# Attention and MLP in one kernel: an earlier score round, and the last stores cut into parts

## The chip, the cores and the metric

The kernel runs on one core of one Trainium2 chip, in one launch. The metric is the device time of an execution in microseconds (us). An execution has a span, from the first to the last instruction that the profiler records, and about two microseconds around it.

## The reference

Eight batches, eight heads of 64 channels, 512 local and 32 global tokens a batch. Local queries see the 32 global keys and the local keys within a window of 32 positions; global queries see everything. The heads' outputs are put side by side (544 rows of 512 channels a batch, 4352 in all), and two matrices with a gated activation between them follow.

```python
s_g  = scale * q_g @ concat(k_g, k_l).T ;  out_g = sm(s_g) @ concat(v_g, v_l)
s_ll = where(|i - j| <= 32, scale * q_l @ k_l.T, -1e9)
s_lg = scale * q_l @ k_g.T
out_l = sm(concat(s_lg, s_ll)) @ concat(v_g, v_l)
x = concat(out_g, out_l) as [4352, 512]
h = x @ w_in                      # 512 -> 2048
out = (h * sigmoid(1.702 * h)) @ w_out    # 2048 -> 512, float32
```

## The kernel before

Operands are bf16, sums float32. The order in which each engine works is the order in which the program names the steps; there is no scheduler behind it. Each engine runs its own list, and waits are put in from the tiles that are written and read.

**Attention** of a batch is done in two *quads* of four heads, `a` and `c` in the code (class `Wide` from batch 1 on). A quad has these steps:
- `S(0)`, `S(1)`: the scores in two rounds, 24 matmuls each with 32 rows in use at a time (32*128 in the profile, L558), into four PSUM banks of their own (`psS`). Both rounds and all quads share these four banks, so a round waits for the exponentials of the round before it.
- `X(0)`, `X(1)`: exponentials on ScalarE (L569), two instructions a round, into `e`. `M(0)`, `M(1)`: the window's mask is multiplied in on VectorE, or on GpSimd where the code says so (L574).
- `U(0)`, `U(1)`, `U(2)`: 24 matmuls each, tile shape 128*32 (L584). `U(0)` sums the exponentials, `U(1)` and `U(2)` give the products with the values. Each takes one bank `ov`. `Gm` (20 matmuls, L595) gives the global queries' output into a bank `og`. `UG` is these four in a row.
- `R`: VectorE transposes the sums (`sT`, L460), takes reciprocals (L462) and transposes back (`rs`, L464). `XL(0)`, `XL(1)` multiply the `ov` banks by them into the MLP's input `xL` (L469). `G` does the same for the global rows.

**MLP.** For each batch `h_step` runs 16 times (four matmuls into a bank `hp`, L613, then the activation on ScalarE, L618). The second product is done for batches 2 and up in `Pair`s of two tiles of 128 rows, with seven products of eight matmuls (128*128, L724, `mm(k)`) instead of eight; VectorE and ScalarE put them together (`m3`, `z`, `zm`, `sub`, `evict`, `add`), and `store` writes the rows in eight DMAs from SP's queue (L762). A pair uses two banks, `px` and `py`.

The banks `hp`, `ov`, `og`, `px`, `py` and `op` come in turn from one pool of four (`psP`): each takes the bank that the fourth before it used, once that has been read. In `phase_o` the two pairs and the two quads' steps take them in this order: a's three `ov` and `og`, then `px` and `py` of the first pair, c's three `ov` and `og`, then `px` and `py` of the second pair. So c's third `ov` and its `og` go where the first pair's `px` and `py` were, and the second pair's `px` and `py` go where c's first two `ov` were.

`phase_o(i)` runs for batches 2 to 6 between the `h_step` loops of batch i and i+1. It puts the pairs of batch i between the attention steps of batch i+1, and, for i = 2 to 5, starts the first quad `a2` of batch i+2. This last form (`if a2`) is the one that the change touches, and it runs four times. `loads_after` issues the DMAs of the values and keys of later batches on GpSimd's queue, behind its mask multiply.

**The end.** The rows of the 32 global tokens of all batches (256 rows) go through the MLP last (`h_step(B, ...)`, then the code from L1138). Its seven products go into four banks `x0`, `x1`, `y0`, `y1`; the last product, `mm(7)`, adds into `y0`, which VectorE has read before (L1157). The four results, each 128 partitions by 256 channels, are stored as quarters, one DMA of 128 KB each: the first and the last from ScalarE's queue, the second and third from SP's (L757).

Every store adds to one of eight semaphores, which are given out in turn, and waits first for the store before it on the same semaphore.

Of the kernel before, what the change touches and what calls it, by code (L numbers as in the profile page):

```python
# [20 lines left out]
def kernel(  # L21
# [12 lines left out]
    nc = tc.nc  # L34

    B, H, Sl, D = q_l.shape
    Sg = q_g.shape[2]
# [128 lines left out]
    for i in range(2):  # L166
# [3 lines left out]
        out=step, in_=step, pattern=[[1, 289]], compare_op=ALU.is_ge,  # L170
# [105 lines left out]
    out_by_row = out.rearrange("(b s) m -> s b m", b=B)  # L276
# [6 lines left out]
    def spair():  # L283
        return [psS.tile([128, 2, 512], F32, name="s4", tag="s%d" % i) for i in range(2)]

    def bank(pair, j):
        return pair[j // 2][:, j % 2, :]
# [340 lines left out]
    def gelu_table():  # L628
        gelu(spot[:, 0:1], spot[:, 1:2])

    def exp_table():
        nc.scalar.activation(spot[:, 0:1], spot[:, 1:2], AF.Exp)
# [26 lines left out]
    HM = d_model // 2  # L659
# [18 lines left out]
    def g_sums(i, lo, hi, which=(0, 1, 2, 3)):  # L678
        n = width(i)
        if i not in sums:  # L680
            if i < B:
                sums[i] = [moe.tile([128, FC // 2, w * HT], BF16, name="gs%d" % k)
                           for k, w in enumerate((1, 1, 2, 1))]
            else:
                room = [ld.tile([128, 2, 16 * D], BF16, name=x).rearrange("p a b -> p (a b)")
                        for x in ("rk", "rq", "rk")]
                sums[i] = [x.rearrange("p (g t) -> p g t", g=FC // 2)
                           for x in (room[0][:, :1024], room[0][:, 1024:], room[1], room[2][:, :1024])]
        a11, a12, a21, a22 = parts_of(i)
        t = gTs[i].rearrange("p (g e) t -> p g e t", e=2)  # L690
        g = slice(lo, hi)
        for k in which:
            if k == 2:
                nc.vector.tensor_tensor(sums[i][2][:, g, :n], t[:, g, 0, :n], t[:, g, 1, :n], ALU.add)  # L694
            else:
                x, y, op = {0: (a11, a22, ALU.add), 1: (a21, a11, ALU.subtract), 3: (a12, a22, ALU.subtract)}[k]
                nc.vector.tensor_tensor(sums[i][k][:, g, : n // 2], x[:, g], y[:, g], op)  # L697

    class Pair:
# [53 lines left out]
                tile_out(self.i, self.tt + h * (width(self.i) // 256),  # L753
                         self.ob[:, 2 * h : 2 * h + 2].rearrange("p h m -> p (h m)"))

        def quarter(self, h, m, eng):
            eng.dma_start(out=out_by_row[:Sg, 4 * h : 4 * h + 4, m * HM : m * HM + HM], in_=self.ob[:, 2 * h + m])  # L757

    def tile_out(i, tci, ob):
        rows = out[i * S + Sg : (i + 1) * S].rearrange("(r t) m -> t r m", t=16)  # L760
# [12 lines left out]
    a, c = Quad(0), Quad(1)  # L773
# [86 lines left out]
    a, c = nq[1]  # L860
# [63 lines left out]
    a, c = nq[2]  # L924
# [26 lines left out]
    def loads_after(i):  # L951
        if i + 2 < B:
            load_v(i + 2)
        if i == 1:
            load_g(8, NQ)
        if i + 3 < B:
            load(i + 3)

    def quads_of(n):
        if n < B and n not in nq:  # L960
            nq[n] = (Wide(2 * n), Wide(2 * n + 1))
        return nq.get(n, (None, None))
# [44 lines left out]
    def phase_o(i):  # L1007
        b = i + 1
        a, c = nq[b]
        a2, c2 = quads_of(b + 1)  # L1010
        p0, p1 = Pair(i, 0), Pair(i, 1)
        exp_table()
        a.UG()
        c.S(0)
        a.R()
        g_sums(i, 7, 8, (0,))
        a.XL(0)
        g_sums(i, 7, 8, (1, 2))
        a.XL(1)
        g_sums(i, 7, 8, (3,))  # L1020
        p0.mm(3, 4, 1)
        c.X(0)
        p0.m3()
        p0.z()
        a.G()
        c.M(0)
        c.S(1)
        c.X(1)
        p0.mm(6)
        p0.zm()  # L1030
        c.M(1)
        p0.mm(5, 2)
        p0.sub()
        p0.evict()
        p0.mm(7)
        p0.add()
        p0.store()
        if a2:
            c.U(0)
            a2.S(0)  # L1040
            a2.X(0)
            a2.M(0, nc.gpsimd)
            c.U(1)
            c.U(2)
            c.Gm()
            loads_after(i + 1)
        else:
            pt = spair()
            c.U(0, bank(pt, 0))
            c.U(1, bank(pt, 2))  # L1050
            c.U(2, bank(pt, 3))
            c.Gm(bank(pt, 1))
        c.R()
        c.XL(0)
        if a2:
            c.XL(1)
            c.G()
        p1.mm(3, 4)
        p1.m3()
        p1.z()  # L1060
        if not a2:
            c.XL(1)
            c.G()
        p1.mm(1, 6)
        p1.zm()
        if a2:
            a2.S(1)
            a2.X(1)
        p1.mm(5, 2)
        p1.sub()  # L1070
        p1.evict()
        gelu_table()
        p1.mm(7)
        p1.add()
        if a2:
            a2.M(1)
        p1.store()

    for i in range(1, B):
        if i > 1:  # L1080
            for fc in range(FC):
                h_step(i, fc)
                if i == 2 and fc == 0:
                    weight_sums(1, 2)
                if i + 1 < B:
                    c = nq[i + 1][1]
                    if fc == 1:
                        c.Tk()
                        c.Tq()
                        c.ext((3,))  # L1090
                    if fc in (3, 5, 7):
                        c.ext(((3, 5, 7).index(fc),), on_act)
                    if fc == 9 and i + 2 < B:
                        a2 = quads_of(i + 2)[0]
                        a2.T()
                        transpose_g(2 * i + 4, 2 * i + 6)
                        a2.ext()
                if fc in (4, 8, 12):
                    g_sums(i, fc // 2 - 2, fc // 2)
                if fc == 13:  # L1100
                    g_sums(i, 6, 7)
        if i == 1:
            phase_o1()
        elif i + 1 < B:
            phase_o(i)
# [4 lines left out]
    def pair_banks(k):  # L1110
        return [psX.tile([128, 512], F32, name="x", tag="x%d" % (2 * (k % 2) + j)) for j in range(2)]
# [3 lines left out]
    for st in range(FC):  # L1115
        h_step(B, st)
        if st < len(todo):
            tt, k = todo[st]
            if k == 3:
                p = Pair(B - 1, tt, pair_banks(tt))  # L1120
# [19 lines left out]
    p = Pair(B, 0, (x0, x1, y0, y1))  # L1140
# [7 lines left out]
    p.mm(5)  # L1148
    on_act(p.ob[:, 1], x0[:, :HM])
    nc.vector.tensor_sub(zb, za, x0[:, :HM])  # L1150
    p.quarter(0, 1, nc.scalar)
    p.mm(2)
    on_act(p.ob[:, 2], x1[:, :HM])
    nc.vector.tensor_sub(zc, za, x1[:, :HM])
    p.quarter(1, 0, nc.sync)
    p.mm(1)
    nc.vector.tensor_add(zc, zc, y0[:, :HM])  # L1157
    p.mm(6)
    nc.vector.tensor_add(p.ob[:, 3], zc, y1[:, :HM])
    p.quarter(1, 1, nc.sync)  # L1160
    p.mm(7)
    nc.vector.tensor_add(p.ob[:, 0], zb, y0[:, :HM])
    p.quarter(0, 0, nc.scalar)


# [28 lines left out]
```

## Time and profile before

| | |
|---|---|
| median of 3 runs | 288.9 us (288.88 to 288.94) |
| profiled execution | 288.66 us |
| its span | 286.6 us, 2.06 less than its time |
| granted TensorE clock | 1.0 |
| TensorE busy | 277.6 us, 97% of the span |
| VectorE, ScalarE, GpSimd busy | 204.6, 184.4, 94.1 us |
| one `phase_o` with `a2` (the second) | from 132.33 to about 150.1 us |
| first product of the last rows' end (L724) | from 276.34 us |

In the profile's rows PE is TensorE's matmuls, PEld its weight loads, DVE is VectorE, ACT ScalarE, POOL GpSimd, SP the engine whose queue issues most stores (SPq, and ACTq for ScalarE's queue). A row gives start and length in microseconds, then engine, line, operation, the tile written and the tiles read; in brackets how long the engine had been idle and what ended it. The chain of waits follows the work back from the last instruction; "x24" counts the instructions that were recorded, of which a few can be missing.

### The profile page before, as it was taken

What the parts mean: (1) busy time and instruction counts of PE and PEld (TensorE: products, weight loads), DVE (VectorE), ACT (ScalarE), POOL (GpSimd) and SP (SyncE); (2) the same over time, 40 slices, a digit from 0 to 9 for tenths busy, and PEclk for the clock granted to TensorE, in tenths of its full rate; (3) what the DMA queues carried; (4) which work ended last, traced back from release to release, by engine and by line L of the source; (5) the groups of instructions that cost most, each with busy time, mean ns of one, the idle gap of its engine ahead of it and who ended that gap; (6) DMA issues with size and microseconds to landing.
All of it is one profiled execution on the core that took longest, in us unless ns stands there. A gap on an engine that the chain in (4) does not pass through costs nothing.

```text
span 286.6 us, 8822 instructions
## 1 busy us (share of the span) xinstructions
PE 277.6 (97%) x3704; PEld 178.6 (62%) x3727; DVE 204.6 (71%) x494; ACT 184.4 (64%) x296; POOL 94.1 (33%) x140
## 2 busy tenths in 40 slices
PE   7899999999999999999999999999999999999994
PEld 6544445544554488646884588647874588458883
DVE  7671457788689898679957997779957697363452
ACT  4847657388778784778559774877658761873440
POOL 8974550766936002920086004800040000000000
PEclk9999999999999999999999999999999999999999
DMA  7999994999999802993059703940122003200213
GB/s 204 167 200 211 202 143 66 153 224 144 161 170 174 150 3 57 91 185 59 12 84 160 139 2 78 107 58 5 29 54 70 2 3 76 73 0 2 73 44 106
DMA packets 59543, 28.23 MB, mean 98 GB/s; under 512 B 47472, under 2 KB 50032, under 8 KB 59504
## 3 DMA queue, kind: packets, MB, share of 16 engines
q0 software_dynamic: 51664, 17.57, 55.1%
q1 hardware_dynamic: 7264, 9.31, 11.8%
q10 hardware_dynamic: 576, 0.79, 0.8%
q8 instruction: 29, 0.48, 0.7%
q14 instruction: 10, 0.08, 0.1%
HBM read 36.31 MB, written 8.91 MB: 158 GB/s over the span
## 4 chain that ended last, share of the span: by engine, by line
PE 91%; DVE 2%; DMA 2%; POOL 1%; issue 1%; ACT 1%; DVEq 0%; POOLq 0%
PE hp L613 38%; PE px L724 13%; PE py L724 9%; PE op L653 9%; PE x L724 6%; PE s L558 6%; PE ov L584 5%; PE s L613 2%; DMA rk<-in_k_l_dram 2%; DVE xL L469 1%; ACT e L382 1%; PE og L595 1%; DVE rs L464 1%; DVE sT L460 0%; PE s L354 0%
## 5 line engine op out<-in xcount | busy, mean ns | idle before, releaser
L613 PE MATMUL hp<-xL,w_in_sb 128*128 128x512 bf16 x465 | 104.6, 379 | 1.2 <-DVE xL L469 0.4
L613 PEld LDWEIGHTS <-w_in_sb 128*128 128x128 bf16 x576 | 56.1, 98 | 60.3 <-issue 0.7
L618 ACT ACTIVATE gT<-hp 128x512 bf16<-128x512 f32 x120 | 69.9, 598 | 20.8 <-PE hp L613 19.3
L569 ACT ACTIVATE e<-s 128x1016 bf16<-128x1016 f32 (+1 forms) x56 | 53.3, 1003 | 22.1 <-PE s L558 22.0
L724 PEld LDWEIGHTS <-gs 128*128 128x128 bf16 x480 | 46.2, 98 | 6.4
L697 DVE TENSOR_TENSOR gs<-gT 128x512 bf16<-128x512 bf16 (+1 forms) x90 | 30.4, 365 | 17.6 <-ACT gT L618 17.3
L574 POOL TENSOR_TENSOR e<-e,mask 128x1760 bf16<-128x1760 bf16 x4 | 13.3, 3320 | 82.6 <-ACT e L569 82.6
L98 POOL DMA_DIRECT2D v<-in_v_l_dram x40 | 31.2, 781 | 15.4 <-PE og L595 4.3
L724 PE MATMUL py<-wsum,gs 128*128 128x256 bf16 x240 | 30.3, 273 | 0.0
L574 DVE TENSOR_TENSOR e<-e,mask 128x1712 bf16<-128x1712 bf16 (+1 forms) x24 | 25.2, 1049 | 6.0 <-ACT e L569 5.9
L653 PE MATMUL op<-w_out_sb,gT 128*128 128x512 bf16 x122 | 28.8, 380 | 0.5 <-issue 0.3
L510 DVE STREAM_TRANSPOSE kT<-rk 128x512 f32<-128x512 f32 x14 | 14.6, 1044 | 15.3 <-DMA rk<-in_k_l_dram 15.3
L653 PEld LDWEIGHTS <-gT 128*128 128x128 bf16 x128 | 11.8, 98 | 13.9
L724 PEld LDWEIGHTS <-gT 128*128 128x128 bf16 x192 | 18.0, 98 | 2.7
L724 PE MATMUL px<-w_out_sb,gT 128*128 128x256 bf16 x160 | 19.2, 273 | 0.0
L724 PE MATMUL px<-w_out_sb,gs 128*128 128x256 bf16 x160 | 19.1, 273 | 0.0
L469 DVE TENSOR_TENSOR xL<-ov,rs 128x512 bf16<-128x512 f32 x27 | 17.9, 687 | 0.8 <-PE ov L436 0.4
L694 DVE TENSOR_TENSOR gs<-gT 128x1024 bf16<-128x1024 bf16 (+1 forms) x30 | 17.4, 580 | 0.0
L558 PEld LDWEIGHTS <-kT 32*128 32x128 bf16 x672 | 12.6, 93 | 7.3 <-issue 5.9
L113 ACT ACTIVATE ob<-px 128x512 f32<-128x512 f32 x10 | 6.0, 599 | 15.2 <-DVE zz L746 15.2
L558 PE MATMUL s<-q,kT 32*128 32x160 bf16 (+1 forms) x448 | 14.9, 246 | 0.0
L100 POOL DMA_DIRECT2D v<-in_v_g_dram x24 | 13.9, 580 | 1.8 <-DMA rq<-in_q_l_dram 1.7
(149 smaller groups left out, 343.4 us busy)
## 6 DMA issues: line engine op xcount, KB each, us to landing
out_dram<-ob SPq DMA_DIRECT2D x128, 64.0 KB, 2.3
rq<-in_q_l_dram POOLq DMA_DIRECT2D x5, 512.0 KB, 8.4
rk<-in_k_l_dram POOLq DMA_DIRECT2D x5, 512.0 KB, 10.6
v<-in_v_l_dram POOLq DMA_DIRECT2D x24, 96.0 KB, 4.7
w_in_sb<-in_moe_w_in_dram POOLq DMA_DIRECT2D x8, 256.0 KB, 8.2
w_out_sb<-in_moe_w_out_dram POOLq DMA_DIRECT2D x4, 512.0 KB, 10.4
rq<-in_q_l_dram POOLq DMA_DIRECT2D x5, 256.0 KB, 7.9
rk<-in_k_l_dram POOLq DMA_DIRECT2D x5, 256.0 KB, 7.9
```

What stands on the lines that cost most here:

```text
L98: nc.gpsimd.dma_start(out=vt[0:n, hs, c, :D], in_=vs[FIRST[c] : FIRST[c] + n, hs])
L469: nc.vector.tensor_mul(self.x[:, 2 * self.u + h, :], self.st[1 + h], self.st["rs"])
L510: nc.vector.transpose(flat[:, 0:Sl].rearrange("p (r t) -> p t r", t=16), loaded[self.b][0][:, self.u].bitcast(F32))
L558: nc.tensor.matmul(bank(self.ps, j)[:, at : at + n], lhsT=self.k[p, KEYS[c] : KEYS[c] + 128, e], rhs=qs[p, :, :, e], start=(e == 0), stop= ...
L569: nc.scalar.activation(self.E[rnd][:, 2 * i : 2 * i + 2, :n], self.ps[i][:, :, :n], AF.Exp, scale=scale)
L574: eng.tensor_mul(e, e, mask[:, rnd : rnd + 1, :n].to_broadcast([128, 4, n]))
L613: nc.tensor.matmul(hp[:, : width(i)], lhsT=w_in_c[:, fc // 4, kc, fc % 4 // 2, :, fc % 2], rhs=(xL[i] if i < B else xG)[:, kc, :], start=( ...
L618: nc.scalar.activation(out_, in_, AF.Gelu_apprx_sigmoid)
L653: nc.tensor.matmul(op, lhsT=gTs[i][:, fc, tci * 128 : tci * 128 + 128], rhs=w_out_sb[:, fc, :], start=(first and fc == 4 * f4), stop=(fc = ...
L694: nc.vector.tensor_tensor(sums[i][2][:, g, :n], t[:, g, 0, :n], t[:, g, 1, :n], ALU.add)
L697: nc.vector.tensor_tensor(sums[i][k][:, g, : n // 2], x[:, g], y[:, g], op)
L724: nc.tensor.matmul(out_, lhsT=lv[:, g, tt * 128 : tt * 128 + 128], rhs=rv[:, g, :], start=(g == 0 and k in ((1, 3, 4, 6) if self.apart els ...
```

## The change

`quarter` takes a list of queues and cuts its DMA into as many parts, by rows of each batch's 32 (8 rows in a quarter's part, 16 in a half). The first quarter becomes four parts, all on SP's queue; the second two, both on ScalarE's; the third two, the first on SP's, the second on ScalarE's; the last two, the first on ScalarE's and the second on SP's. In all ten DMAs instead of four.

In `phase_o` with `a2`, `a2.S(0)` and what follows it (`X`, and `M` on GpSimd) stand ahead of all of c's `UG`, instead of between its `U(0)` and `U(1)`. On TensorE the 24 matmuls of `S(0)` come before the 24 of `U(0)`; the order on the other engines stays.

```diff
-        def quarter(self, h, m, eng):
-            eng.dma_start(out=out_by_row[:Sg, 4 * h : 4 * h + 4, m * HM : m * HM + HM], in_=self.ob[:, 2 * h + m])
+        def quarter(self, h, m, *engs):
+            n = Sg // len(engs)
+            for j, eng in enumerate(engs):
+                eng.dma_start(out=out_by_row[n * j : n * j + n, 4 * h : 4 * h + 4, m * HM : m * HM + HM],
+                              in_=self.ob[4 * n * j : 4 * n * j + 4 * n, 2 * h + m])
...
         if a2:
-            c.U(0)
             a2.S(0)
             a2.X(0)
             a2.M(0, nc.gpsimd)
-            c.U(1)
-            c.U(2)
-            c.Gm()
+            c.UG()
             loads_after(i + 1)
...
-    p.quarter(0, 1, nc.scalar)
+    p.quarter(0, 1, *4 * [nc.sync])
...
-    p.quarter(1, 0, nc.sync)
+    p.quarter(1, 0, nc.scalar, nc.scalar)
...
-    p.quarter(1, 1, nc.sync)
+    p.quarter(1, 1, nc.sync, nc.scalar)
...
-    p.quarter(0, 0, nc.scalar)
+    p.quarter(0, 0, nc.scalar, nc.sync)
```

## The prediction

> **What bounds the kernel now.** I read the page first, then the chain of waits in order of time, then the timeline around the two edited places, then the DMA issues.
>
> ```profile
> span 286.6 us, 8822 instructions
> PE 277.6 (97%) x3704; PEld 178.6 (62%) x3727; DVE 204.6 (71%) x494; ACT 184.4 (64%) x296; POOL 94.1 (33%) x140
> PE 91%; DVE 2%; DMA 2%; POOL 1%; issue 1%; ACT 1%; DVEq 0%; POOLq 0%
> ```
>
> TensorE is the bound from end to end; an edit counts only if it shortens TensorE's own row of work, makes it wait, or moves what follows its last matmul. First edit, first of its four places, in the chain (start, length, what):
>
> ```profile
> 108.70 0.87 PE py L724 x8
> 109.57 0.48 PE ov L584 x24
> 110.05 0.58 PE s L558 x22
> 110.63 0.84 PE ov L584 x40
> 111.47 0.16 PE og L595 x20
> 111.63 1.85 PE px L724 x16
> ```
>
> From the end of py to the start of px, TensorE alone takes 2.06 us: U(0), S(0), U(1) and U(2), Gm. The same gap is 2.05 to 2.06 at 141.16, 172.74 and 204.31. The batch-1 phase already has the new order, S then the whole UG:
>
> ```profile
> 74.59 0.57 PE s L558 x24
> 75.17 1.22 PE ov L584 x66
> 76.38 0.16 PE og L595 x17
> 76.54 0.32 PE op L653
> ```
>
> That is 76.54 - 74.59 = 1.95 us. What VectorE does behind these, from the timeline (start, length, engine, line, what):
>
> ```profile
> 110.28 0.71 DVE L460 STREAM_TRANSPOSE sT<-ov 128x512 f32<-128x512 f32 x1
> 111.56 1.92 PE L724 MATMUL px<-w_out_sb,gT 128*128 128x256 bf16 x16
> 112.13 1.29 DVE L469 TENSOR_TENSOR xL<-ov,rs 128x512 bf16<-128x512 f32 x2
> ```
>
> And the end of the kernel:
>
> ```profile
> 280.33 0.39 ACT L113 ACTIVATE ob<-x 128x256 f32<-128x256 f32 x1 [0.74 <-PE x L724]
> 281.27 0.42 DVE L1157 TENSOR_TENSOR ob<-ob,x 128x256 f32<-128x256 f32 x1
> 281.75 0.75 PEld L724 LDWEIGHTS <-rk 128*128 128x128 bf16 x7 [0.18 <-issue]
> 282.82 0.42 DVE L1162 TENSOR_TENSOR ob<-ob,x 128x256 f32<-128x256 f32 x1 [0.60 <-PE x L724]
> 283.27 0.55 ACTq L757 DMA_DIRECT2D out_dram<-ob  x1
> ```
>
> ```profile
> out_dram<-ob SPq DMA_DIRECT2D x8, 64.0 KB, 1.7
> out_dram<-ob ACTq DMA_DIRECT2D x2, 128.0 KB, 2.2
> out_dram<-ob SPq DMA_DIRECT2D x2, 128.0 KB, 2.1
> ```
>
> The last store is issued at 283.27, lands about 2.1 later (285.37), and 1.2 us of closing follow.
>
> **Edit 1, S(0) ahead of all of UG, four phases.** Nothing is added; 24 matmuls move past the 24 of U(0). TensorE changes between its tile shapes (128*128, 128*32, 32*128) four times in this stretch now, three times afterwards. Gain by the rows: 2.06 - 1.95 = 0.11 us a phase, if nothing makes TensorE wait. What could:
>
> S(0) needs the score banks that the exponentials of c's second round leave at 106.01 + 1.89 = 107.90; it starts at 109.50. U(0) needs the mask multiply that ends at 107.93 + 1.05 = 108.98. U(2) and Gm reuse the banks of the first px and py, free at 110.21 (ScalarE's eviction) and 110.36 (VectorE's add); U(2) comes at about 110.86. All covered, by 0.5 us or more. ScalarE's exponentials start at 110.24 instead of 110.66, still behind that eviction, so GpSimd's mask multiply and the v loads queued behind it go 0.4 us earlier; nobody waits for them.
>
> R is the thin place. Its transpose waits for U(0), which now comes one S(0) later. At 81.28 and 75.10, with S in front, the transpose starts 0.60 after U(0)'s first matmul; S to U(0) is 0.57. So it starts at 109.50 + 0.57 + 0.60 = 110.67, not 110.28 (where VectorE itself was busy until then): R and both XL go 0.39 later. The second px goes into U(0)'s bank and waits for that transpose: 110.67 + 0.71 + 0.06 of handover (VectorE ends at 281.69, TensorE goes on at 281.75) = 111.44, against a natural start of 109.50 + 1.95 = 111.45. No wait. The second py goes into U(1)'s bank and waits for XL(0): its start follows the transpose's by 1.85 (112.13 - 110.28), its length is 0.69 where L469 stands alone, so 110.67 + 1.85 + 0.69 + 0.06 = 113.27, against a natural start of 113.32 - 0.11 = 113.21. A wait of 0.06 takes half of the gain. Left: 0.05 to 0.06 a phase, 0.24 us in four. Bounds: 0.11 x 4 = 0.44 gained (no wait); and, if the handover costs 0.16 as the bubble at 48.53 between U and op does, about 0.05 lost per phase, 0.2 in all. VectorE's later z is covered: it idles 0.85 us before zm at 115.27.
>
> **Edit 2, the four quarters.** (a) The first quarter's issue leaves ScalarE, where it takes 0.66 us (279.62 to 280.28) in front of the next eviction. That eviction can follow its matmul by 0.09, as the one at 279.21 does: 280.08 instead of 280.33. VectorE's chain behind it moves by 0.25, L1157 ends at 281.44 instead of 281.69, and the 0.18 us that TensorE stands before its last eight matmuls goes. L1162 ends at 283.07, not 283.24: 0.17 gained at this point.
>
> (b) The stores. In the program as built each store adds to one of eight semaphores, and first waits for the former store on its semaphore. The eight were given out in an order in which ScalarE's two parts of the second quarter stand before the third and fourth part of the first quarter on SP:
>
> ```
> SP   8x4x256   [waits DMAHW1, Activation]   part 1 of first quarter
> SP   8x4x256   [waits DMAHW2]               part 2
> SP   8x4x256   [waits DMAHW4]               part 3
> SP   8x4x256   [waits DMAHW5]               part 4
> SP   16x4x256  [waits DMAHW6, DVE]          half of third quarter
> SP   16x4x256  [waits DMAHW7, DVE]          half of fourth quarter
> ACT  16x4x256  [waits DMAHW4, Activation]   half of second quarter
> ACT  16x4x256  [waits DMAHW5]               other half
> ```
>
> The wait values say that parts 3 and 4 wait until ScalarE's two halves have landed. Queued on SP behind them: half of the third and half of the last quarter, whose landing ends the kernel. The trace of before has such a wait once (SP on an earlier store, 0.9 us). Step by step: ScalarE issues its halves after its eviction, at 280.08 + 0.39 + 0.02 = 280.50. A store of 128 rows took 0.65 to 0.66 to issue as the first of its shape on a queue and 0.54 to 0.55 as the second; one of 32 rows about 0.43; I take 0.58 and 0.47 for 64 rows. Second half issued at 281.08. Landing: 64 KB takes 1.6 to 1.8, 128 KB 2.1 to 2.4; I take 1.80, nearer the first, since the bytes are the same: 282.88. Part 4 then starts at about 282.92, is issued by 283.35, the third quarter's half by 283.95, and the last half is issued at 283.97 although its data is there at 283.07. It lands 1.75 later: 285.72 against 285.37, so **0.35 us later**, with (a) already in it. ScalarE's last half goes at 283.10 and lands before that. SP's first two parts find their semaphores free.
>
> On these halves the Trainium skill speaks against the change (DMA: Bandwidth & Descriptors, section "Rules for kernel authors": two transfers to disjoint partition halves serialize, so use one). By the fit on the same page (about 2.0 us and bytes / 436 GB/s, made on GpSimd's queue) an estimate for 64 KB is 2.15 us; with both landings at that the end would come 1.10 later instead of 0.35, which is the slower rival's side below. The trace's own 64 KB stores, at 1.7, do not agree.
>
> **Sum.** -0.24 + 0.35 = +0.11 us on the profiled execution: 288.66 becomes 288.77. The median of the runs is 0.24 higher (288.9), so 289.0. What a measurement of this kernel can tell from no change is about 0.2%, 0.58 us; this lies inside.
>
> **Rivals.**
> *Slower: halves cost what wholes cost.* One mechanism, SP's wait for ScalarE's landings, at whole-store prices: halves issued from 280.50, 0.66 each step, landing 2.2: 281.16 + 2.2 = 283.36; part 4 0.43; half of the third 0.65; last half issued at 284.50, landing 2.1 later: 286.60, 1.23 late; less 0.24: +1.0, 289.9 us. For it: the fixed part of a store is most of its time (1.7 against 2.2 for half the bytes). Against: the 64 KB rows. It decides the verdict once the two landings together exceed my 3.55 by some 0.5. Chance 0.25.
> *Faster: SP's wait is short and the phases keep their whole gain.* Halves at 32-row prices: second issued at 280.93, landed (1.6) at 282.53; part 4 by 282.98, half of the third by 283.42, last half lands at 285.04: 0.33 early; with 0.44 from the phases -0.77, 288.1 us. Chance 0.13.
> *Phases give nothing:* the dearer handover (0.16) makes the second py late, +0.2 with +0.35: 289.5 us, mostly inside 0.2%. Chance 0.12.
> *It does not do what it says:* the score round does move in the built program; "by both queues" holds only in name, since SP waits for ScalarE's stores. That is in my sum.
>
> **How the numbers follow.** My forecast has 0.5. Of it and the third rival some 0.06 lies above +0.58. Faster: 0.13; slower: 0.25 + 0.06 = 0.31; same: 0.56. The likeliest is 289.0; the range of 288.3 to 289.9 takes in the bounds of the phases and the slow rival's price, and leaves out what lies beyond it and most of the fast rival.
>
> **What the profile after would show.** Right: gaps of 1.95 to 2.01 from py's end to the second px, with a bubble of some 0.05 before the second py; sT about 0.4 later in each phase; ScalarE's last-but-one eviction 0.25 earlier and no 0.18 before the last matmuls; SP's store parts 3 and 4 at about 282.5 and 282.9 (less 0.24 for what came before), SP's last issue later than ScalarE's by 0.9. Wrong: SP's parts follow each other without a break and the last store is issued right behind L1162 (then faster), or the gap is 2.06 or more (then edit 1 gave nothing), or landings above 2.1 us (then slower).

## The result, and the profile after

| | before | after |
|---|---|---|
| median | 288.95 us (14 runs) | 289.76 us (14 runs) |
| ratio after to before | | 1.003, 95% interval 1.002 to 1.004 |
| profiled execution, its span | 288.66, 286.6 us | 291.09, 289.0 us |

The change makes the kernel 0.8 us slower, just beyond what can be told from no change. The profiled execution of after is one of its longest: its batch-2 phase begins 1.53 us later than before (102.28 against 100.75) and its chain at the start runs through loads that the change does not touch. So the two traces are compared piece by piece, each from its own start.

The chain of waits in order of time, first of the four phases (start, length, what):

```profile
110.24 0.87 PE py L724 x8
111.11 0.57 PE s L558 x24
111.69 1.20 PE ov L584 x63
112.89 0.16 PE og L595 x18
113.05 1.85 PE px L724 x16
114.90 1.82 PE py L724 x16
```

From py's end to px's start: 113.05 - 111.11 = 1.94 us instead of 2.06. The 0.12 lies in UG: its `ov` matmuls take 1.20 in one row, and 0.48 and 0.84 where S(0) stands between them. That a change of tile shape less is what saves it fits these rows; no run tests it by itself. The 16 matmuls of py that follow take 1.82 instead of 1.75. The same two figures stand in the other three phases (1.94 and 1.82 in each). Net 0.05 a phase. Counted from the start of the first of the four to the start of the phase behind them, this trace gives less: 228.54 - 102.28 = 126.26 against 227.07 - 100.75 = 126.32, 0.06 in all, partly because the second phase's first `ov` matmuls, which the change does not touch, take 1.29 instead of 1.20. The timeline shows where the 0.07 comes from:

```profile
112.21 0.72 DVE L460 STREAM_TRANSPOSE sT<-ov 128x512 f32<-128x512 f32 x1 [0.32 <-PE ov L584]
...
112.98 1.92 PE L724 MATMUL px<-w_out_sb,gT 128*128 128x256 bf16 x16
...
114.07 1.29 DVE L469 TENSOR_TENSOR xL<-ov,rs 128x512 bf16<-128x512 f32 x2
114.63 1.81 PEld L724 LDWEIGHTS <-gs 128*128 128x128 bf16 x16
114.81 1.91 PE L724 MATMUL py<-wsum,gs 128*128 128x256 bf16 x16
```

R's transpose now waits for U(0) (0.32 us of idling). It starts 1.17 after S(0)'s first matmul (111.04); px is not held up, since the transpose ends at 112.93 and px starts at 112.98. py stands still until XL(0), 0.69 long, is done: 114.07 + 0.69 = 114.76, start 114.81.

The end, first the engines, then the issues of SP one by one, the last of the eight stores ahead (L765) and the six of the quarters (L759):

```profile
280.67 0.38 ACT L113 ACTIVATE ob<-x 128x256 f32<-128x256 f32 x1 [1.41 <-DMA out_dram<-ob]
...
281.50 0.38 ACT L113 ACTIVATE ob<-x 128x256 f32<-128x256 f32 x1 [0.44 <-PE x L724]
281.82 4.90 SPq L759 DMA_DIRECT2D out_dram<-ob  x6
281.91 3.21 ACTq L759 DMA_DIRECT2D out_dram<-ob  x4
...
282.44 0.42 DVE L1157 TENSOR_TENSOR ob<-ob,x 128x256 f32<-128x256 f32 x1
...
284.12 0.42 DVE L1162 TENSOR_TENSOR ob<-ob,x 128x256 f32<-128x256 f32 x1 [0.45 <-PE x L724]
```

```profile
281.29 0.44 SPq L765 DMA_DIRECT2D out_dram<-ob  x1
...
281.82 0.84 SPq L759 DMA_DIRECT2D out_dram<-ob  x1
...
282.71 0.69 SPq L759 DMA_DIRECT2D out_dram<-ob  x1
...
283.95 0.65 SPq L759 DMA_DIRECT2D out_dram<-ob  x1
...
284.65 0.66 SPq L759 DMA_DIRECT2D out_dram<-ob  x1
...
285.42 0.62 SPq L759 DMA_DIRECT2D out_dram<-ob  x1
...
286.14 0.58 SPq L759 DMA_DIRECT2D out_dram<-ob  x1
```

The last data are ready at 284.12 + 0.42 = 284.54. ScalarE issues its half of the last quarter at 284.57. SP issues the other half at 286.14, **1.60 us after the data**; before it was 0.03. The hole between 283.40 and 283.95 is the wait for ScalarE's first half (issued at 281.91), which the view of SP's waits lists:

```profile
SPq L759 <- DMA out_dram<-ob: 0.5, 1, 0.5
```

Part four, which by the program waits for ScalarE's second half, follows part three at once (283.95 + 0.65 = 284.60, start 284.65). The first part does not start when its data are ready, at 280.67 + 0.38 = 281.05, but 0.77 later, right behind the eight stores of the last pair that SP had still to issue (281.29 + 0.44 = 281.73). The prediction does not have this; by these rows it costs nothing here, since part three waits for ScalarE's landing either way.

From the last vector instruction's end to the end of the span: 289.0 - 284.54 = 4.46 us, before 286.6 - 283.24 = 3.36. That is 1.10 more. Ahead of it the pause of 0.18 before the last eight matmuls is gone (the last 24 matmuls take 2.78 instead of 2.95). Sum by the pieces: -0.05 x 4 - 0.17 + 1.10 = +0.73, or +0.87 with the 0.06 that the four phases gave in this trace; measured +0.81.

### The profile page after: what moved, and what is told of

It is laid out like the page before. It is cut to its first block, busy times and chain, and to the rows that moved or that the text cites. A ratio compares the mean times of both kernels' runs of the same rounds, so it can differ in the third digit from the quotient of the medians.

```text
span 289.0 us, 8853 instructions
## 1 busy us (share of the span) xinstructions
PE 280.4 (97%) x3727; PEld 179.8 (62%) x3727; DVE 205.0 (71%) x494; ACT 184.2 (64%) x296; POOL 94.0 (33%) x140
## 4 chain that ended last, share of the span: by engine, by line
PE 89%; DMA 4%; ACT 2%; DVE 2%; SPq 0%; issue 0%; POOL 0%
PE hp L613 36%; PE px L724 13%; PE py L724 9%; PE op L653 9%; PE x L724 6%; PE s L558 6%; PE ov L584 5%; DMA rk<-in_k_l_dram 3%; DMA early<-in_q_l_dram 2%; PE s L613 1%; ACT e L382 1%; PE og L595 1%; PE s L354 1%; ACT e L385 1%; PE s L337 1%; ACT gT L618 0%
## 5 line engine op out<-in xcount | busy, mean ns | idle before, releaser
L653 PE MATMUL op<-w_out_sb,gT 128*128 128x512 bf16 x128 | 29.5, 380 | 0.0
```

The costliest lines, as they stand in the source:

```text
L653: nc.tensor.matmul(op, lhsT=gTs[i][:, fc, tci * 128 : tci * 128 + 128], rhs=w_out_sb[:, fc, :], start=(first and fc == 4 * f4), stop=(fc = ...
```

## The experiments

All times are medians, with the ratio to the kernel before on the same chip and its 95% interval. "End" is the time from the end of the last vector instruction to the end of the span, and "last issue" the time from there to the start of the last store's issue, both from each run's trace.

### Each edit alone

The score round moved, the four stores as before:

```diff
-    p.quarter(0, 1, *4 * [nc.sync])
+    p.quarter(0, 1, nc.scalar)
-    p.quarter(1, 0, nc.scalar, nc.scalar)
+    p.quarter(1, 0, nc.sync)
-    p.quarter(1, 1, nc.sync, nc.scalar)
+    p.quarter(1, 1, nc.sync)
-    p.quarter(0, 0, nc.scalar, nc.sync)
+    p.quarter(0, 0, nc.scalar)
```

> Only the score round is moved; the four stores are as before. Theory (one change of tile shape less on TensorE, half of it given back by py's wait for XL(0)): each of the four phases 0.04 to 0.05 us shorter, the gap from py's end to px's start 1.94, py 0.07 late; 0.2 us less in all, 288.75 against 288.95, which is at the edge of what can be told. Rival (the earlier round costs elsewhere, in the loads or the loops): 289.2 or more.

288.83 us, 0.9994 (0.9984 to 1.0003). The trace has the expected pieces (1.93 to 1.94 from py to px, py 1.82), and the four phases from start to start take 126.17 us, 0.15 less than before. The time agrees with -0.2 but can't be told from nothing, and the rival's 289.2 is out.

The stores alone, the phases as before:

```diff
-            a2.S(0)
...
-            c.UG()
+            c.U(0)
+            a2.S(0)
...
+            c.U(1)
+            c.U(2)
+            c.Gm()
```

> Only the stores are changed; the phases are as before. Theory (the end alone makes the change slower): from the last vector instruction to the end of the span 4.4 to 4.5 us instead of 3.36, the last product 0.17 earlier; 0.9 us more, 289.85. Rival (the moved round is to blame): 289.0.

289.96 us, 1.0036 (1.0023 to 1.005). End 4.45, last issue 1.58 after the data. The stores alone make the kernel as slow as the whole change does, within the intervals.

### What holds SP's last issue back

Whole quarters on swapped queues, both edits otherwise as in the change:

```diff
-    p.quarter(0, 1, *4 * [nc.sync])
-    p.quarter(1, 0, nc.scalar, nc.scalar)
-    p.quarter(1, 1, nc.sync, nc.scalar)
-    p.quarter(0, 0, nc.scalar, nc.sync)
+    p.quarter(0, 1, nc.sync)
+    p.quarter(1, 0, nc.scalar)
+    p.quarter(1, 1, nc.sync)
+    p.quarter(0, 0, nc.scalar)
```

> Both edits, but each quarter stored whole: first on SP, second on ScalarE, third on SP, fourth on ScalarE, four DMAs as before. Theory (the number of issues on SP is what costs, and taking the first issue off ScalarE is worth 0.17): the last store issued right behind the last vector instruction, 3.36 us to the end as before; 0.2 from the phases and 0.17 less, 288.6. Rival (SP's backlog of eight stores holds the first and third quarter up): third quarter issued late, 288.95 or more.

288.73 us, 0.9988 (0.9977 to 0.9999). End 3.40, last issue 0.04 after the data, although SP's first store again starts behind its earlier ones (280.39, its data ready at 279.62). The last 56 matmuls take 6.13 us, and 6.28 in the run with the order alone: moving the first issue off ScalarE takes the pause away in the trace, but the time can't be told from 288.83. So it is not the other queue that made the end late; it is the cut.

The second quarter issued from GpSimd, so that SP waits for no store of ScalarE's:

```diff
-    p.quarter(1, 0, nc.scalar, nc.scalar)
+    p.quarter(1, 0, nc.gpsimd, nc.gpsimd)
```

> As the changed kernel, but the second quarter's two halves are issued from GpSimd, so that no store of SP's waits for a store of ScalarE's; SP still issues its six. Theory of the prediction (SP's wait for ScalarE's landings is most of the delay): the last store issued within 0.2 us of the last vector instruction, some 1.4 us earlier than in the changed kernel, 288.5. Rival (six issues of 0.6 to 0.8 us one after another are most of it, whatever they wait for): SP's six follow each other from 281.8 without a break, the last at about 285.6 instead of 286.14; 0.5 us less than the changed kernel, 289.3.

289.14 us, 1.0004 (0.9996 to 1.0013). The timeline's last vector instruction and SP's six issues:

```profile
281.15 4.38 SPq L759 DMA_DIRECT2D out_dram<-ob  x6
...
283.45 0.42 DVE L1162 TENSOR_TENSOR ob<-ob,x 128x256 f32<-128x256 f32 x1 [0.45 <-PE x L724]
```

Without the wait the six still fill 4.38 us, 0.58 to 0.84 each, and the last starts at 284.96, 1.09 after the data instead of 1.60. The rival was right: the wait is 0.5 of the delay, and the row of six issues, which begins 0.76 after the first quarter's data (280.39), is enough for the rest.

The first quarter's parts cut by batch, everything else as in the change:

```diff
+            if len(engs) == 4:
+                for j, eng in enumerate(engs):
+                    eng.dma_start(out=out_by_row[:Sg, 4 * h + j, m * HM : m * HM + HM],
+                                  in_=self.ob[j : 128 : 4, 2 * h + m])
+                return
```

> As the changed kernel, but the first quarter's four parts are cut by batch (32 rows of one batch each) instead of by rows (8 rows of four batches each); same bytes, queues, number and waits. Theory (an issue's price goes with the pattern, three dimensions against two, and not with the bytes): the first two parts take 0.43 us each to issue instead of 0.84 and 0.69, the last store is issued 0.3 to 0.4 earlier, 289.4. Rival (the price goes with SP and ScalarE issuing at the same time): 0.6 to 0.8 as before, 289.76.

289.87 us, 1.0025 (1.0016 to 1.0035). The same 32 KB now take 0.58, 0.58, 0.47 and 0.47 us to issue instead of 0.84, 0.69, 0.65 and 0.66, so the price goes with the pattern, if less than expected. The time did not move:

```profile
280.60 3.38 SPq L760 DMA_DIRECT2D out_dram<-ob  x4
...
282.90 0.42 DVE L1167 TENSOR_TENSOR ob<-ob,x 128x256 f32<-128x256 f32 x1 [0.45 <-PE x L724]
284.08 1.40 SPq L764 DMA_DIRECT2D out_dram<-ob  x2
```

The third part starts at 282.88 and the fourth at 283.51, just when ScalarE's halves (issued at 280.69 and 281.38) have landed, 2.2 and 2.1 us later. What was saved was waited. The last issue is at 284.93, 1.61 after the data. The expected 0.3 to 0.4 was a miss, because I had left the waits out of it.

Both together:

```diff
+            if len(engs) == 4:   # the four parts by batch, as above
...
-    p.quarter(1, 0, nc.scalar, nc.scalar)
+    p.quarter(1, 0, nc.gpsimd, nc.gpsimd)
```

> As the changed kernel, with both: the first quarter's four parts cut by batch, and the second quarter issued from GpSimd. Theory (two limits of nearly the same length lie on top of each other in the changed kernel, SP's issues and its wait for ScalarE's landings, so that taking away either one alone brings little): with both gone SP's last issue comes 0.2 to 0.3 us after the last vector instruction instead of 1.6 and 1.1; 0.8 less than with GpSimd alone, 288.4. Rival (something else holds SP's queue): 289.0 or more.

288.59 us, 0.9977 (0.9965 to 0.999).

```profile
280.92 2.49 SPq L760 DMA_DIRECT2D out_dram<-ob  x4
...
283.22 0.42 DVE L1167 TENSOR_TENSOR ob<-ob,x 128x256 f32<-128x256 f32 x1 [0.45 <-PE x L724]
283.51 1.27 SPq L764 DMA_DIRECT2D out_dram<-ob  x2
```

The last issue is at 284.21, 0.57 after the data. The price alone brought nothing, the wait alone 0.5, both 1.0: two limits of nearly the same length lay on top of each other. A gap of 0.57 is left where I expected 0.2 to 0.3, since the parts took 0.58 to 0.60 each, back to back. The first of them also started 0.75 after its data (280.92 against 280.17), behind SP's earlier stores. That is more than the gap, but no run takes it away.

The first quarter whole on SP, the other three cut as in the change:

```diff
-    p.quarter(0, 1, *4 * [nc.sync])
+    p.quarter(0, 1, nc.sync)
```

> As the changed kernel, but the first quarter is one store on SP; the other three stay in two parts on both queues. Theory (SP's serial issues of the four parts, and their wait, are the whole delay): SP is free before the third quarter is ready, the last half is issued within 0.1 us of the last vector instruction instead of 1.6, about 1.3 us less than the changed kernel, 288.5. Rival (cutting the last two quarters costs as such, by issues or by contention): 289.2 or more.

288.81 us, 0.9992 (0.9981 to 1.0003). Last issue 0.03 after the data (283.48 against 283.45). With three issues less on SP the whole delay is gone. The wait went with them: the view of SP's waits lists no DMA for the quarters here, so this run takes both limits away at once. The end is 3.45, no better than with whole quarters.

### Does cutting the last store help by itself

```diff
-    p.quarter(0, 0, nc.scalar)
+    p.quarter(0, 0, nc.scalar, nc.sync)
```

(on the kernel with whole quarters)

> As the kernel with whole quarters on swapped queues, but the last quarter is stored in two halves, one from ScalarE and one from SP. Theory (a half lands 0.1 us sooner than a whole, both are issued at the same time, one semaphore less follows): 0.1 to 0.15 less, 288.6. Rival (the two halves run on the same engines and land together no sooner than the whole): 288.7 to 288.8.

288.79 us, 0.9991 (0.9981 to 1.0001): no different from the 0.9988 with whole quarters. The 0.1 to 0.15 of the theory did not come, and the rival was right. In the trace both halves are issued at 282.75 and 282.76; SP's lands 2.0 later, ScalarE's 2.2, where a whole quarter took 2.1, and the end is 3.57 instead of 3.40. Here the trace agrees with the rule of the Trainium skill that the prediction cited (DMA: Bandwidth & Descriptors, "Rules for kernel authors"): halves on two queues do not land sooner.

### The order in which SP waits at the end

In the change 0.86 us pass from the last landing (286.14 + 2.0) to the end of the span, before 1.23 (283.27 + 2.1); landings and spans are read to 0.1 us. In the program as built, SP waits at the end for the eight semaphores in the order 0 to 7. The last store had number 1 before and 7 after. To test it, six more stores are issued earlier, off the path, which hands the numbers on by six:

```diff
-            nc.sync.dma_start(out=rows[4 * tci + j], in_=ob[32 * j : 32 * j + 32])
+            for g in ((slice(0, 16), slice(16, 32)) if (i, tci) in ((4, 0), (4, 2)) and j < 3 else (slice(0, 32),)):
+                nc.sync.dma_start(out=rows[4 * tci + j][g], in_=ob[32 * j : 32 * j + 32][g])
```

On the kernel with whole quarters:

> As the kernel with whole quarters on swapped queues, but three 64 KB stores of each of two tiles of batch 4 are cut in two, so that the eight semaphores are handed on by six places and the last store has the one that SP waits for last. Theory (SP takes the eight semaphores in a fixed order at the end, some 0.06 us each, so those that come after the last landing are paid): from the last landing to the end of the span 0.86 us instead of 1.23; 0.35 less than with whole quarters, 288.4. Rival (the closing time has nothing to do with it): 288.7.

288.23 us, 0.9969 (0.9958 to 0.998). From the landing (283.47 + 2.1) to the end (286.5): 0.93 instead of 1.26. This is the fastest of the versions here, faster than both kernels: the score round moved, quarters whole on swapped queues, the last store on the last semaphore.

On the kernel before, with nothing else changed:

> The kernel before, with nothing of the change; only three 64 KB stores of each of two tiles of batch 4 are cut in two, so that its last store has the semaphore that SP waits for last. Theory (waits behind the last landing are paid, six of them): from the last landing to the end 0.9 instead of 1.23; 0.33 less, 288.65. Rival (the gain of the kernel with whole quarters and shifted semaphores came from elsewhere): 288.95.

288.68 us, 0.9984 (0.9971 to 0.9996). From landing (283.75 + 2.1) to the end (286.8): 0.95 instead of 1.23. It is the semaphore's place, with the stores of before and with the swapped queues.

### What py waits for

c's R without the reciprocals and the second transpose, in the four phases, so that XL multiplies by the sums themselves. The kernel ran once; its trace is read, its time is not compared:

```diff
+            if short:
+                self.st["rs"] = sT.rearrange("p a b -> p (a b)")
+                return
...
-        c.R()
+        c.R(bool(a2))
```

> As the changed kernel, but in the four phases c's R leaves out the reciprocals and the second transpose (the inputs of XL are the transposed sums, so the output is not the reference's). Theory (py waits for XL(0), which R makes late): XL(0) starts about 1.1 us earlier, px to py and py itself without a bubble, the 16 py matmuls 1.75 us in the chain instead of 1.82. Rival (the 0.07 comes with the tile shapes or the weight loads): 1.82 stays.

The chain of waits:

```profile
111.82 1.85 PE px L727 x16
113.67 1.75 PE py L727 x16
```

py takes 1.75 again, in all four phases, with XL(0) 1.04 earlier (1.92 after the start of S(0) in the chain, 2.96 in the change). Tile shapes and weight loads are as in the change. So the 0.07 is the wait for XL(0), and it takes back more than half of the 0.12 that the order gains.

## Why the prediction was right or wrong

The sign of the forecast's difference and its mechanism held, and the range held the time. The size did not: +0.1 was forecast, which could not have been told from no change, and +0.8 came, which can. So the side that came is the slower one, to which I had given 0.31, and not the likeliest (0.56).

*Edit 1.* Right step by step: the gap of 1.95 (1.94), R's transpose 1.17 after S(0)'s start (1.17), px not held up, py held up by 0.06 (0.07). By these pieces it comes to about 0.2 in four phases, as forecast 0.24. From start to start the phases gave 0.06 in the profiled execution and 0.15 in the run with the order alone, so the gain may be smaller, and the times can't tell.

*Edit 2 (a).* Right: the second eviction follows its matmul sooner, the pause before the last product is gone, 0.17 us.

*Edit 2 (b).* The mechanism was right: SP's parts stand behind a landing of ScalarE's, and the halves queued behind them are late. Its terms were mis-sized. Counted from ScalarE's first issue, part four began 0.32 later than forecast (2.74 instead of 2.42): that issue took 0.65 instead of 0.58, its store landed about 2.0 later instead of 1.80, and part three, itself held up by the landing, took 0.65. From part four to the last issue it was 1.49 instead of 1.05. The step that failed there is the price of an issue: 0.43 for a part, because the 64 KB stores of 32 rows by 2 KB took 0.43. The parts measured 0.65 to 0.84, and about 0.1 passed between one issue and the next where the sum had 0.02. I had scaled with size, and the row that was nearest in pattern, not in bytes, was the 128 KB quarter (0.54 to 0.66). The forecast's 0.58 to 0.60 for a half was about right (0.58 and 0.62). All this put the last issue 1.60 us after the data instead of 0.90. Then the last half's landing was taken as 1.75 and measured 2.0.

The other way went the closing, 0.37 shorter, which the sum did not have: the prediction lists the semaphores, but not the order in which they are waited for at the end. 0.70 + 0.25 - 0.37 = 0.58, and with 0.04 from the phases the forecast's +0.11 becomes the +0.73 that the pieces of the trace give. That the range held the time was luck to this extent: without the shorter closing the time would have been about 290.1 us, above the range.

*The rivals.* "Halves cost what wholes cost" gave +1.0 and came nearest. Its price of an issue, 0.65 to 0.66, was nearly that of the halves and of the last parts, though it too had 0.43 for a part; its landings (2.2 and 2.1) were a little dear. Its condition, the two landings together some 0.5 above 3.55, came about (2.0 and 2.0). But it named the wait as the one mechanism, and with the wait taken away (GpSimd) most of the delay stayed: removing the landings' hold on SP alone is worth 0.5 of 1.6. The sign that the prediction named for it, landings above 2.1 us, did not show, and the kernel was slower all the same. "Faster" fell with the price of the issues, "phases give nothing" with the trace.

## What to carry to other kernels

Count the issues on a queue as work in a row: with five small stores queued ahead of it, the last one goes when the queue is free, not when its data are ready, and cutting a store by bytes did not cut the time to issue it here. Before one of two waits is blamed, take both away; where they overlap, either alone shows little. Look at which semaphores stores share across queues and in which order they are waited for at the end, since both are set by counting and not by what the code says.

## What the runs showed that I had not expected

The price to issue a store goes with its pattern more than with its bytes. At the end of the kernel it was 0.42 to 0.44 us for 32 rows of 2 KB (64 KB), 0.65 to 0.84 for 8 rows of 4 batches by 1 KB (32 KB), 0.47 to 0.60 for 32 rows of one batch by 1 KB (the same 32 KB), 0.55 to 0.81 for 16 rows of 4 batches by 1 KB (64 KB) and 0.54 to 0.67 for the 128 KB quarter. Why one and the same pattern took 0.47 in one place and 0.60 in another stays open. There, 64 KB landed in 1.7 to 1.8 as rows of 2 KB and in 1.9 to 2.3 as rows of 1 KB. And about 0.3 us at the end hung on the number of the last store's semaphore, in kernels that differ in nothing else at their end.
